# New places for the routing matmuls among the expert matmuls, and one copy moved from ScalarE to VectorE

## The chip, the cores and the metric

The kernel runs on one core of one Trainium2 chip. The metric is the device time of one execution in microseconds, as a median of three runs. One core has five engines that run their own queues in order: TensorE (PE in the rows, its weight loads PEld), VectorE (DVE), ScalarE (ACT), GpSimd (POOL) and SyncE (SP, which here only issues transfers).

## The reference

Three layers follow one another on 4 x 768 = 3072 tokens of width 512. First a decaying linear attention with 8 heads of 64. Then a dense feed-forward layer, and last a layer of 8 experts:

```python
h = x @ w_in                                   # 512 -> 2048
g = h * np.tanh(softplus(h))
x = g @ w_out                                  # 2048 -> 512
logits = x @ w_gate                            # 8 experts
order = np.argsort(-logits.flatten())
for idx in order:                              # best pairs first
    tok, e = (int(idx) // E, int(idx) % E)
    if assigned[tok] >= 0 or counts[e] >= cap: # cap = 3072 / 8 = 384
        continue
    assigned[tok] = e
    counts[e] += 1
for e in range(E):
    mask = assigned == e
    out[mask] = np.maximum(x[mask] @ w1[e], 0.0) @ w2[e]
```

Every expert gets exactly 384 tokens, and which expert is filled first depends on all logits.

## The kernel before, in words

All large products are done in half precision with a high and a low part of each operand, three matmuls for each product (`mm3`, L524). The last part of the kernel, from the logits on, is what matters here. Three kinds of work run in it side by side.

The **routing** is done in eight rounds (`route_round`). Each round finds the expert that fills up next, by a search over the digits of the logits. A round r has five digit steps. In each, VectorE compares (`against`, L677, into the tile `ld`), TensorE counts with 24 small matmuls (tile `pc{r}x{0,2,4,6,8}x`, L720), VectorE thresholds (L722), TensorE spreads the result with one matmul (tile `pn{r}x{1,3,5,7,9}x`, L725), and VectorE takes the maximum (L727) and prepares the next digit (L731, L732, L734, L677). Then VectorE closes the round: it finds the number of the expert (up to L760), TensorE makes prefix sums (`pp{r}x10x`, L769 and L770), VectorE takes the chosen tokens out of the logits (up to L784), and the next round begins with L687. A side chain (`route_list`) makes the list of the 384 tokens, with 24 small matmuls (`pl{r}x11x`, L812). Rounds are strictly one after the other.

The **weights** of the expert that round r has found are fetched by two indirect transfers of 2 MB (`weights`, L855, `w1p` and `w2p`), which need the number from L760. ScalarE sums their squares (four times L861 for each), TensorE and VectorE make a scale from it (`pt{r}x2x` for w1, `pt{r}x3x` for w2, L184, L186), and ScalarE, GpSimd and VectorE split each of the eight pieces of 128x1024 into high and low parts (L213, L215, L221, L222, L227, L228).

The **experts** (`expert`) are the matmuls themselves. Expert r starts when its tokens are gathered (`prep_x`, L883) and its w1 is split. It makes eight groups of 12 matmuls of 128x384 (first half) and three groups of 24 matmuls of 128x512 (second half), into the accumulators `ph` and `px` by turns. Each group of the first half is followed by VectorE (L914), ScalarE (L915) and GpSimd (L916).

In what order TensorE and ScalarE do all this is fixed when the program is written out: `Weave` counts a planned time, adds the planned cost of each piece of main matmuls, and lets a side chain issue its next step when its planned wait has passed. For the routing, this wait is a constant of the step plus an entry of the table `KN['rs']`, one row for each round: entries 0 to 9 stand ahead of the ten matmul steps `pc`, `pn`, `pc`, ..., entry 10 ahead of `pp` and entry 11 ahead of `pl`:

```python
yield max(0.0, KN['rw'][i] + (4 if i == 0 else 1) * slack + rs[2 * i]), 0.0
pc = ps.tile([128, E], F32, name=f"pc{r}x{2 * i}x", tag="py")
```

A larger entry puts the step behind more expert matmuls in TensorE's queue. TensorE takes its queue in order: where a routing matmul stands too early, TensorE waits for VectorE with expert matmuls behind it; where it stands too late, VectorE waits. The orders of VectorE and GpSimd are made by the scheduler from the dependences.

Expert 0's tokens are special: they are transposed by TensorE (L895, three accumulators `ph`, `px`, `ph`) and copied to the tile `xt` (L897 and L899). Those of the later experts are transposed by transfers.

Of the kernel before, what the change touches and what calls it, by code (L numbers as in the profile page):

```python
# [16 lines left out]
AF = mybir.ActivationFunctionType  # L17
# [80 lines left out]
def moe_kernel(ctx, tc, qkv, w_in, w_out, w_gate, w1p, w2p,  # L98
               c_mask, c_g, c_gv, c_gs, out, dbg=None):
    nc = tc.nc  # L100
    V, A, P, T, SY = nc.vector, nc.scalar, nc.gpsimd, nc.tensor, nc.sync
# [60 lines left out]
    def first_loads():  # L162
        for x in KN['lo']:
            if x[0] == 'c':
                load_chunk(0, int(x[1]), 3 if x == 'c0' else 1)
            elif x == 'g':
                SY.dma_start(GQ, c_g)
                SY.dma_start(GV, c_gv)
            elif x == 'm':
                SY.dma_start(MASK, c_mask)  # L170
            elif x == 's':
                SY.dma_start(GS, c_gs)
            elif x == 'wg':
# [103 lines left out]
    def win_setup(q):  # L277

        zs = [RAW[:, i * 1024:i * 1024 + 1024] for i in (2 * q, 2 * q + 1)]
        for j in range(2):  # L280
            with tc.high_priority(offset=KN['cp'][q]):
              to_f32(zs[j], WIN_RAW[2 * q + j], KN['ci'][2 * q + j])
            if 2 * q + j < 3:
                win_load(2 * q + j + 5)
        yield KN['wv'][0], 0.0
        yield KN['wv'][1], 1.0
        ss = col("ssi")
        norm(zs, ss)
        yield KN['wv'][2], 0.2
        sw = pow2(total(ss, 1, "toti"), "swin", 4)  # L290
# [544 lines left out]
    def ps_any():  # L835
        return next(banks)()
# [41 lines left out]
    def prep_x(r):  # L878
        xt = wk.tile([128, 2, KD, G], F16, name="xt", tag="xt", bufs=2)
        XTE_[r] = xt  # L880
        for c in range(CPG):
            xg = XG[(r % 2) * CPG + c]
            P.indirect_dma_start(out=xg, out_offset=None, in_=xbuf,  # L883
                                 in_offset=bass.IndirectOffsetOnAxis(ap=IDX[r][:, c:c + 1], axis=0))
            if r:
                turned(xt, c, xg[:, :2 * DM])
        if r == 0:

            yield 10.0, 0.0
# [12 lines left out]

# [173 lines left out]
    wv = Weave(tc)  # L1076
# [133 lines left out]
```

## Time and profile before

| | |
|---|---|
| median of 3 runs | 1168.45 us (1164.66 to 1170.23) |
| the profiled execution's own time | 1161.92 us |
| its span, first to last instruction | 1160.1 us |
| mean granted clock of TensorE | 0.926 of full speed |
| TensorE busy | 990.7 us, 85% |
| VectorE, ScalarE, GpSimd busy | 71%, 55%, 50% |

The profile is of one execution, whose time lies 6.5 us under the median. The span is 1.8 us shorter than this execution's time. Times in the rows count from the first instruction. "Granted clock" is the share of 2.4 GHz at which TensorE was allowed to run; its two levels are 1.2 and 2.4 GHz. The brackets at the end of a row give the idle time of the engine just before and who ended it.

### The profile page before, as it was taken

What the parts mean: (1) busy time and instruction counts of PE and PEld (TensorE: products, weight loads), DVE (VectorE), ACT (ScalarE), POOL (GpSimd) and SP (SyncE); (2) the same over time, 40 slices, a digit from 0 to 9 for tenths busy, and PEclk for the clock granted to TensorE, in tenths of its full rate; (3) what the DMA queues carried; (4) which work ended last, traced back from release to release, by engine and by line L of the source; (5) the groups of instructions that cost most, each with busy time, mean ns of one, the idle gap of its engine ahead of it and who ended that gap; (6) DMA issues with size and microseconds to landing.
All of it is one profiled execution on the core that took longest, in us unless ns stands there. A gap on an engine that the chain in (4) does not pass through costs nothing. (4 is left out here: it accounts for less than half of the span.)

```text
span 1160.1 us, 19911 instructions
## 1 busy us (share of the span) xinstructions
PE 990.7 (85%) x7897; PEld 565.1 (49%) x7897; DVE 818.3 (71%) x1766; ACT 641.3 (55%) x942; POOL 585.7 (50%) x415
## 2 busy tenths in 40 slices
PE   3458768899999999999999899994888788869997
PEld 2335444445556555555565464442444444435553
DVE  6899989853777667767867465786878788695320
ACT  4336857563567575675675672153445454556741
POOL 5956463641445536335544232033476665767872
PEclk9959979889999999999999999995888889889999
DMA  9360361273130231131341100516252535527600
GB/s 302 127 185 18 137 172 29 74 138 71 47 94 17 83 74 46 37 83 47 83 79 42 37 1 20 200 28 197 91 167 82 146 119 182 154 74 182 200 28 28
DMA packets 108814, 113.67 MB, mean 98 GB/s; under 512 B 92464, under 2 KB 92592, under 8 KB 106672
## 3 DMA queue, kind: packets, MB, share of 16 engines
q1 hardware_dynamic: 102576, 66.24, 22.4%
q0 software_dynamic: 6144, 46.15, 11.6%
q8 instruction: 62, 1.02, 0.4%
q14 instruction: 32, 0.26, 0.1%
HBM read 77.50 MB, written 13.64 MB: 79 GB/s over the span
## 5 line engine op out<-in xcount | busy, mean ns | idle before, releaser
L524 PE MATMUL ph<-xt,WIN 128*128 128x384 f16 x1728 | 335.9, 336 | 7.3 <-DMA xt<-yh 3.8
L524 PE MATMUL px<-WOUT,G 128*128 128x512 f16 x1248 | 315.2, 388 | 0.2 <-DVE WOUT L228 0.2
L524 PEld LDWEIGHTS <-WIN 128*128 128x128 f16 x1920 | 188.9, 102 | 154.4 <-issue 29.7
L524 PEld LDWEIGHTS <-G 128*128 128x128 f16 x1728 | 166.5, 100 | 193.7 <-issue 20.8
L576 POOL TENSOR_TENSOR G<-RAW,G 128x1536 f16<-128x1536 f32 (+1 forms) x32 | 99.5, 3108 | 103.2 <-DVE G L573 87.2
L405 POOL TENSOR_TENSOR amt<-amt 128x512 f16<-128x512 f32 x40 | 55.7, 1393 | 121.6 <-DVE amt L402 104.9
L916 POOL TENSOR_TENSOR G<-G,G 128x384 f16<-128x384 f32 x64 | 64.7, 1017 | 70.3 <-ACT G L915 65.6
L554 DVE TENSOR_SCALAR RAW<-ph 128x384 f32<-128x384 f32 x124 | 68.1, 551 | 40.5 <-PE ph L524 39.9
L915 ACT ACTIVATE G<-G 128x384 f16<-128x384 f32 x64 | 33.0, 519 | 89.7 <-DVE G L914 89.1
L561 ACT ACTIVATE RAW<-RAW,zt,ch 128x1536 f32<-128x1536 f32 x32 | 53.3, 1665 | 48.5 <-DVE RAW L554 43.0
L324 ACT ACTIVATE junk<-ld 128x512 bf16<-128x512 f32 x63 | 39.4, 626 | 62.0 <-DMA ld<-in_qkv_dram 61.0
L570 DVE TENSOR_TENSOR RAW<-RAW 128x1536 f32<-128x1536 f32 (+1 forms) x33 | 60.6, 1837 | 15.5 <-ACT RAW L569 15.4
L222 POOL TENSOR_TENSOR RAW<-ld,RAW 128x512 f16<-128x512 f32 x34 | 45.6, 1357 | 50.9 <-ACT RAW L221 45.9
L861 ACT ACTIVATE junk<-RAW 128x1024 bf16<-128x1024 f32 x64 | 67.1, 1048 | 6.7 <-DMA RAW<-in_w1p_dram,MASK 6.0
L677 DVE TENSOR_TENSOR ld<-MASK,ld 128x1536 bf16<-128x1536 bf16 (+1 forms) x35 | 56.5, 1614 | 0.7
L222 POOL TENSOR_TENSOR STH<-SC,STH 64x256 f16<-64x256 f32 x34 | 32.0, 942 | 42.2 <-ACT STH L221 39.1
L524 PEld LDWEIGHTS <-WOUT 128*128 128x128 f16 x384 | 38.7, 104 | 27.5 <-issue 6.1
L399 DVE TENSOR_TENSOR amt<-pa,MASK 128x512 f32<-128x512 f32 x38 | 26.1, 688 | 35.1 <-PE pa L398 30.6
L524 PE MATMUL px<-WIN,G 128*128 128x512 f16 x192 | 44.3, 380 | 5.8 <-POOL G L916 3.1
L720 PEld LDWEIGHTS <-ld 128*128 128x128 bf16 x840 | 24.8, 97 | 49.7 <-DVE ld L677 46.8
L222 POOL TENSOR_TENSOR WIN<-RAW,WIN 128x1024 f16<-128x1024 f32 x19 | 45.3, 2389 | 5.5 <-ACT WIN L221 5.3
L569 ACT ACTIVATE RAW<-RAW 128x1536 f32<-128x1536 f32 (+1 forms) x33 | 47.7, 1445 | 0.4
(585 smaller groups left out, 2145.5 us busy)
## 6 DMA issues: line engine op xcount, KB each, us to landing
ld<-in_qkv_dram SPq DMA_DIRECT2D x20, 768.0 KB, 4.9
G<-in_w_in_dram SPq DMA_DIRECT2D x8, 1024.0 KB, 8.5
G<-in_w_out_dram SPq DMA_DIRECT2D x8, 1024.0 KB, 5.3
x_rows<-xr SPq DMA_DIRECT2D x24, 256.5 KB, 2.8
G<-in_qkv_dram SPq DMA_DIRECT2D x2, 768.0 KB
g_columns<-G SPq DMA_DIRECT2D x1, 1024.0 KB
G<-g_columns SPq DMA_DIRECT2D x1, 1024.0 KB
ld<-in_qkv_dram SPq DMA_DIRECT2D x3, 256.0 KB, 2.8
```

Of the source, the lines that this page charges most:

```text
L222: (V if pool in ("V", "E") else P).tensor_tensor(lo, src, hi, op=OP.subtract)
L324: A.activation(junk(), x.rearrange("p a d -> p (a d)"), AF.Square, accum_out=ss[:, i:i + 1])
L405: (P if mode[1] == "P" else V).tensor_tensor(amh[:, j, 1], am, amh[:, j, 0], op=OP.subtract)
L524: T.matmul(p, a, b, start=i == 0, stop=i == n - 1)
L554: V.tensor_scalar(hs[:, f], p[:, :G], 1.0 / 65536.0, None, op0=OP.mult)
L561: A.activation(th, hs, AF.Tanh, scale=ch[:, q:q + 1], bias=z)
L569: A.activation(th[:, w], th[:, w], AF.Sin, scale=-2.0, bias=math.pi / 2)
L570: (V if hm[1] == 'V' else P).tensor_tensor(th[:, w], th[:, w], hs[:, w], op=OP.mult)
L576: (P if lo == 'P' else V).tensor_tensor(gb[:, 1, o], th[:, w], gb[:, 0, o], op=OP.subtract)
L677: V.tensor_tensor(out.rearrange("p t (j v) -> p t j v", v=VR), cv[:, ts, None, :].to_broadcast([128, n, J // VR, VR]), RT["jr128"][:, :J]. ...
L861: A.activation(junk(1024), RAW[:, o:o + 1024], AF.Square, accum_out=ss[:, j:j + 1])
L916: P.tensor_tensor(hid[:, 1, f], hs, hid[:, 0, f], op=OP.subtract)
```

## The change

Two things are changed. The rows 0 to 7 of the table `rs` get new entries, 67 of 96; and all three copies of expert 0's transposed tokens are done by VectorE, where ScalarE did the second one. The row of round 3 shows the size of the first:

```diff
-rs=[...
-[0.56, 0.0, 0.38, 0.0, 0.15, 0.0, 0.12, -0.11, -0.04, -0.27, 0.03, -3.34],
+rs=[...
+[1.97, 0.0, -0.9, -0.59, 4.52, 0.43, 0.84, -0.56, 3.53, 0.17, -0.61, -4.08],
...
-                if c == 1:
-                    A.activation(xt[:, :, :, c * C:(c + 1) * C], p, AF.Copy)
-                else:
-                    V.tensor_copy(xt[:, :, :, c * C:(c + 1) * C], p)
+                V.tensor_copy(xt[:, :, :, c * C:(c + 1) * C], p)
```

The number of instructions and their operands stay the same on TensorE; only places differ. In the changed kernel the lines behind L896 have numbers that are 3 lower.

**First place: TensorE, round 3, from the spreading matmul of the second digit to the counting matmuls of the third.** The first column of names is the accumulator, with its running number. Before:

```order
L725 MATMUL pn3x3x_9375<-MASK_83,onesb_77 128x8
L524 LDWEIGHTS G1_68
L524 MATMUL px_9320<-WIN_64,G1_68 128x512
...
L524 MATMUL ph_9394<-xt_9022,WOUT_65 128x384
L720 LDWEIGHTS ld_7847
L720 MATMUL pc3x4x_9410<-MASK_83,ld_7847 128x8
```

After the change:

```order
L725 MATMUL pn3x3x_9390<-MASK_83,onesb_77 128x8
L524 LDWEIGHTS WOUT_65
L524 MATMUL ph_9385<-xt_8994,WOUT_65 128x384
...
L524 MATMUL px_9456<-xt_8994,WOUT_65 128x384
L720 LDWEIGHTS ld_7847
L720 MATMUL pc3x4x_9472<-MASK_83,ld_7847 128x8
```

Before, 4 matmuls of 128x512 and 12 of 128x384 stood between the two; now 44 of 128x384 do, the last of them for the fourth group of expert 1.

**Second place: the weights of expert 6.** GpSimd issues the transfers, and TensorE's matmuls `pt6x2x` and `pt6x3x` sum the squares of w1 and w2. GpSimd before, from the issue for w1 to the issue for w2:

```order
L855 DMA RAW_66<-in_w1p_dram,MASK_83 128x4096
L916 TENSOR_TENSOR G1_68<-G0_67,G1_68 128x384 x3
L215 TENSOR_SCALAR RAW_66<-RAW_66,se1_11271 128x1024 x2
L222 TENSOR_TENSOR WOUT_65<-RAW_66,WOUT_65 128x1024
L916 TENSOR_TENSOR G1_68<-G0_67,G1_68 128x384
L222 TENSOR_TENSOR WOUT_65<-RAW_66,WOUT_65 128x1024 x2
L883 DMA G0_67<-x2_rows,GQ_81 128x1026 x3
L933 DMA out_0_dram<-G0_67,GQ_81 3072x512
L855 DMA RAW_66<-in_w2p_dram,MASK_83 128x4096
```

GpSimd after (L913 is the line that was L916):

```order
L855 DMA RAW_66<-in_w1p_dram,MASK_83 128x4096
L913 TENSOR_TENSOR G1_68<-G0_67,G1_68 128x384 x2
L855 DMA RAW_66<-in_w2p_dram,MASK_83 128x4096
L913 TENSOR_TENSOR G1_68<-G0_67,G1_68 128x384
```

TensorE after, where expert 6 begins:

```order
L812 LDWEIGHTS amt_7848
L812 MATMUL pl7x11x_11665<-GQ_81,amt_7848 128x6
L184 MATMUL pt6x2x_11692<-sse0_11412,onesf_79 128x4
L184 MATMUL pt6x3x_11706<-sse1_11414,onesf_79 128x4
L524 LDWEIGHTS WIN_64
L524 MATMUL px_11730<-xt_11628,WIN_64 128x384
```

The two issues now stand next to each other, and both sums stand directly ahead of expert 6's first matmul. Before, `pt6x2x` stood among the first groups of expert 5 and `pt6x3x` in its second half.

**Third place: VectorE, the copies of expert 0's tokens.** Before, with ScalarE's copy of `px` (L897) in another queue:

```order
L899 COPY xt_8735<-ph_8851 128x8x128
L734 TENSOR_TENSOR MASK_83<-MASK_83 128x192
L191 TENSOR_SCALAR se0a_8844<-tote_8842 128x1
L923 TENSOR_SCALAR GQ_81<-G0_67,ie_8696 128x1
L677 TENSOR_TENSOR ld_7847<-MASK_83,ld_7847 128x24x64
L899 COPY xt_8735<-ph_8871 128x8x128
```

After:

```order
L896 COPY xt_8735<-ph_8840 128x8x128
L734 TENSOR_TENSOR MASK_83<-MASK_83 128x192
L896 COPY xt_8735<-px_8850 128x8x128
L677 TENSOR_TENSOR ld_7847<-MASK_83,ld_7847 128x24x64
L896 COPY xt_8735<-ph_8860 128x8x128
```

The scale of expert 1's weights (L191), which stood between the copies, now comes behind them.

## Rows read from the trace of the kernel before

**Rows 1.** The page, busy time of the engines over the span.
```profile
PE 990.7 (85%) x7897; PEld 565.1 (49%) x7897; DVE 818.3 (71%) x1766; ACT 641.3 (55%) x942; POOL 585.7 (50%) x415
```

**Rows 2.** Windows: length; busy PE, PEld, DVE, ACT, POOL; granted clock, DMA share, GB/s.
```profile
797.00:1060.00 263.00, 214.47 (x1640) 113.73 (x1640) 203.43 (x541) 126.26 (x188) 165.20 (x121) 0.86 0.45 134
1060.00:1147.00 87.00, 86.02 (x468) 45.41 (x466) 27.93 (x49) 51.32 (x77) 61.75 (x50) 1.00 0.37 113
```

**Rows 3.** Waits of TensorE, 797 to 1060 us: total, times, longest.
```profile
PE px L524 <- ACT xt L897: 4.0, 1, 4.0
PE pc3x4x L720 <- DVE ld L677: 4.0, 1, 4.0
...
PE pc6x4x L720 <- DVE ld L677: 2.2, 1, 2.2
```

**Rows 4.** Timeline of TensorE, around the third digit of round 3.
```profile
858.24 0.80 PE L720 MATMUL pc3x4x<-MASK,ld 128*128 128x8 bf16 x24 [4.00 <-DVE ld L677]
...
859.32 2.72 PE L524 MATMUL px<-xt,WOUT 128*128 128x384 f16 x8
861.98 0.18 PE L725 MATMUL pn3x5x<-MASK,onesb 64*128 64x8 bf16 x1
```

**Rows 5.** Timeline of TensorE, the last groups of expert 7.
```profile
1134.38 2.11 PE L524 MATMUL px<-xt,WOUT 128*128 128x384 f16 x12
1136.33 5.34 PE L524 MATMUL ph<-WOUT,G 128*128 128x512 f16 x24
1141.51 5.34 PE L524 MATMUL px<-WOUT,G 128*128 128x512 f16 x24
1146.68 5.34 PE L524 MATMUL ph<-WOUT,G 128*128 128x512 f16 x24
```

**Rows 6.** Timeline of all engines where expert 0 begins.
```profile
803.60 0.69 DVE L899 COPY xt<-ph 128x1024 f16<-128x1024 f16 x1 [1.13 <-PE ph L895]
...
805.44 1.00 ACT L897 ACTIVATE xt<-px 128x1024 f16<-128x1024 f16 x1
...
806.50 4.00 PE L524 MATMUL px<-xt,WIN 128*128 128x384 f16 x12 [4.01 <-ACT xt L897]
...
811.57 0.81 PE L720 MATMUL pc2x4x<-MASK,ld 128*128 128x8 bf16 x24
```

**Rows 7.** Timeline of TensorE, the last digit step of rounds 2, 5 and 6.
```profile
829.21 0.18 PE L725 MATMUL pn2x9x<-MASK,onesb 64*128 64x8 bf16 x1
...
969.09 0.18 PE L725 MATMUL pn5x9x<-MASK,onesb 64*128 64x8 bf16 x1
...
1020.88 0.19 PE L725 MATMUL pn6x9x<-MASK,onesb 64*128 64x8 bf16 x1
```

**Rows 8.** Timeline of GpSimd, the issue of w1 for expert 6.
```profile
1026.68 0.97 POOL L855 DMA_INDIRECT RAW<-in_w1p_dram,MASK  x1 [2.75 <-DVE MASK L760]
```

**Rows 9.** The transfers of L855: from issue to landing.
```profile
DMA to landing us min/median/max: 8.6/8.8/13.0
```

**Rows 10.** Groups by line and form, 797 to 1147 us: count, busy us, mean ns.
```profile
L861 ACT ACTIVATE junk<-RAW 128x1024 bf16<-128x1024 f32 x52 | 54.4, 1047 | 1.2 <-DMA RAW<-in_w1p_dram,MASK 0.7
...
L222 POOL TENSOR_TENSOR WOUT<-RAW,WOUT 128x1024 f16<-128x1024 f32 x18 | 39.8, 2219 | 4.0 <-ACT WOUT L221 3.8
...
L228 DVE SCALAR_TENSOR_TENSOR WOUT<-RAW,se,WOUT 128x1024 f16<-128x1024 f32 x14 | 22.5, 1606 | 5.8 <-ACT WOUT L227 5.7
...
L914 DVE TENSOR_SCALAR G<-ph 128x384 f32<-128x384 f32 x32 | 17.7, 554 | 23.5 <-issue 8.6 <-PE ph L524 8.5 <-POOL G L916 3.2
...
L227 ACT ACTIVATE WOUT<-RAW,se 128x1024 f16<-128x1024 f32 x14 | 15.9, 1138 | 25.2 <-DVE se L194 25.2
```

**Rows 11.** Timeline of all engines, a routing step on VectorE beside GpSimd.
```profile
813.92 2.13 POOL L222 TENSOR_TENSOR WOUT<-RAW,WOUT 128x1024 f16<-128x1024 f32 x1 [1.25 <-ACT WOUT L221]
...
814.39 1.70 DVE L731 SCALAR_TENSOR_TENSOR MASK<-MASK 128x24 bf16<-128x24 bf16 x1
...
824.37 0.26 DVE L731 SCALAR_TENSOR_TENSOR MASK<-MASK 128x24 bf16<-128x24 bf16 x1
```

More of the change, by code (lines that the diff above doesn't have):

```diff
@@ L36 @@
 DIGITS = ((25, 7), (18, 7), (12, 6), (6, 6), (0, 6))
-KN = dict(ea=1, sc=1, pw=4, le=0.0, hl=['P', 'P'], cs=['V', 'V', 'V', 'V', 'V', 'V', 'V'], cc=['V', 'V', 'V', 'V', 'V', 'V', 'V', 'V', 'V'], lo=['c0', 'g', 'c1', 'm', 'c2', 's', 'wg', 'w0', 'w1', 'w2'], ga=['', 'V'], rs=[[-0.63, 0.3, -1.2, 0.0, 0.24, 0.0, 0.09, 0.0, 0.21, 0.0, 0.0, -4.24], [2.1, 0.09, 2.19, 0.0, 0.58, 0.15, 0.18, 0.15, 0.26, 0.26, 1.46, -0.41], [3.26, 0.0, -0.68, 0.2, 0.33, 0.0, -0.3, 0.0, 0.09, -0.12, 0.3, -3.18], [0.56, 0.0, 0.38, 0.0, 0.15, 0.0, 0.12, -0.11, -0.04, -0.27, 0.03, -3.34], [0.67, 0.0, 0.31, -0.76, 0.89, 0.0, 0.15, -0.22, 0.0, 0.0, -0.16, -4.15], [1.46, -2.35, 0.04, -0.29, 0.13, -2.18, 0.42, -0.4, 0.45, 0.03, 1.16, -4.07], [0.45, 0.54, 0.45, 0.0, 1.18, 0.0, -0.39, -0.55, -0.61, -0.05, 0.45, -3.57], [-0.15, 0.0, -0.75, 0.0, 0.0, 0.0, 0.0, -0.3, 0.0, 0.0, 3.28, -3.01]], fs=[[0.0, 0.0, -3.96, -1.22], [-0.75, 0.0, 1.32, 0.16], [0.0, 0.0, -2.08, 0.13], [0.0, -1.13, 0.71, 0.36], [0.0, 0.0, 0.0, -0.56], [0.38, 0.75, 0.13, 0.04], [0.0, 0.38, 0.2, 0.69], [0.0, -1.5, -0.61, 0.29]], av=[5.75, 5.75, 2.0, 4.0], a2=[1.3, 2.2, 4.3], a1=[0.1, 1.0, 0.85], ao=[3.5, 3.5, 3.35], wv=[8.5, 0.5, 1.0, 4.5], ov=5.0, an=[3.0, 3.15, 3.6], qm=['P0', 'VP', 'VP', 'PH', 'P1', 'VV', 'VP'], vm=['P0', 'VP', 'VP', 'VP', 'VP', 'P0', 'VP'], km=['A', 'H', 0, 0, 0, 0, 0], am=['VP', 'VP', 'VP', 'AV', 'VP', 'AV', 'VP'], ss=['V', 'P', 'P', 'P', 'P', 'P', 'P'], sm=['P', 'V', 'V', 'P', 'E', 'D', 'P'], ym=[0, 0, 0], hm=['VVVP', 'VVAV', 'VVVP', 'VVVP', 'AVVP', 'VVVP', 'VVVP', 'VVVP', 'VVVP'], ci=['PP', 'PP', 'AP', 'PP', 'PP', 'PP', 'VP', 'PP'], co=['AP', 'PP', 'PP', 'PP', 'AP', 'PP', 'PP', 'PP'], wa=[15, 12, 8, -1, 7, 16], cp=[0, 100, 0, 100], np=0, yp=[0, 2000], op=[0, 0, 200, 0, 50, 1000], xp=[0, 0, 0, 0, 0, 0], ld=[0, 1, 2, 3, 4], wj=[4, 4, 4], fw=[13.5, 18.5, 14, 16, 14, 16], qs=1.0, tw=3.0, sw=1.5, po=[[0, 1, 0, 1, 0, 0, 0, 1], [0, 'A', 0, 1, 0, 1, 0, 0], [0, 1, 0, 1, 0, 1, 0, 1], [0, 'A', 0, 'A', 'A', 1, 0, 1]], sl=[0, 0, 0.7], rw=[4.9, 2.5, 1.55, 1.7, 1.7], pn=0.5, lw=14.0, gx=9.0, tk=2.75, st=[16.0, 21.0, 20.0, 23.5], wi=['H', 'A', 0, 0, 2, 0, 0, 0], wo=['H', 'H', 0, 0, 0, 0, 'H', 0], tp=[], gw=5.15, nw=1.0, cw=0, sp=50, ap=1000, wp=None, ip=None)
@@ new lines @@
+KN = dict(ea=1, sc=1, pw=4, le=0.0, hl=['P', 'P'], cs=['V', 'V', 'V', 'V', 'V', 'V', 'V'], cc=['V', 'V', 'V', 'V', 'V', 'V', 'V', 'V', 'V'], lo=['c0', 'g', 'c1', 'm', 'c2', 's', 'wg', 'w0', 'w1', 'w2'], ga=['', 'V'], rs=[[-0.17, 0.3, 0.32, 0.0, 0.24, -0.1, 0.09, -0.1, 0.51, -0.1, -0.52, -4.58], [2.1, 1.0, 0.74, 0.0, 0.99, -0.62, 1.08, 2.0, -0.2, 0.16, -0.44, -0.41], [3.26, 0.0, -0.99, 0.2, 0.69, -0.45, 3.77, 0.43, 0.09, -0.57, 0.3, -4.61], [1.97, 0.0, -0.9, -0.59, 4.52, 0.43, 0.84, -0.56, 3.53, 0.17, -0.61, -4.08], [2.13, -0.19, 1.72, -0.76, 4.94, 0.44, -0.63, -0.67, 2.68, 0.44, 0.84, -3.66], [3.09, -0.58, 0.04, -0.99, 0.13, -1.79, 1.61, 0.18, 2.13, -0.42, 3.65, -3.58], [0.95, 0.94, -0.23, -0.7, 3.7, 0.43, -0.39, -0.55, 2.89, 0.38, 0.45, -3.11], [-0.15, 0.0, -0.75, 0.0, 0.0, 0.0, 0.0, -0.3, 0.0, 0.0, 3.91, -6.01]], fs=[[0.0, 0.0, -3.96, -1.22], [-0.75, 0.0, 1.32, 0.16], [0.0, 0.0, -2.08, 0.13], [0.0, -1.13, 0.71, 0.36], [0.0, 0.0, 0.0, -0.56], [0.38, 0.75, 0.13, 0.04], [0.0, 0.38, 0.2, 0.69], [0.0, -1.5, -0.61, 0.29]], av=[5.75, 5.75, 2.0, 4.0], a2=[1.3, 2.2, 4.3], a1=[0.1, 1.0, 0.85], ao=[3.5, 3.5, 3.35], wv=[8.5, 0.5, 1.0, 4.5], ov=5.0, an=[3.0, 3.15, 3.6], qm=['P0', 'VP', 'VP', 'PH', 'P1', 'VV', 'VP'], vm=['P0', 'VP', 'VP', 'VP', 'VP', 'P0', 'VP'], km=['A', 'H', 0, 0, 0, 0, 0], am=['VP', 'VP', 'VP', 'AV', 'VP', 'AV', 'VP'], ss=['V', 'P', 'P', 'P', 'P', 'P', 'P'], sm=['P', 'V', 'V', 'P', 'E', 'D', 'P'], ym=[0, 0, 0], hm=['VVVP', 'VVAV', 'VVVP', 'VVVP', 'AVVP', 'VVVP', 'VVVP', 'VVVP', 'VVVP'], ci=['PP', 'PP', 'AP', 'PP', 'PP', 'PP', 'VP', 'PP'], co=['AP', 'PP', 'PP', 'PP', 'AP', 'PP', 'PP', 'PP'], wa=[15, 12, 8, -1, 7, 16], cp=[0, 100, 0, 100], np=0, yp=[0, 2000], op=[0, 0, 200, 0, 50, 1000], xp=[0, 0, 0, 0, 0, 0], ld=[0, 1, 2, 3, 4], wj=[4, 4, 4], fw=[13.5, 18.5, 14, 16, 14, 16], qs=1.0, tw=3.0, sw=1.5, po=[[0, 1, 0, 1, 0, 0, 0, 1], [0, 'A', 0, 1, 0, 1, 0, 0], [0, 1, 0, 1, 0, 1, 0, 1], [0, 'A', 0, 'A', 'A', 1, 0, 1]], sl=[0, 0, 0.7], rw=[4.9, 2.5, 1.55, 1.7, 1.7], pn=0.5, lw=14.0, gx=9.0, tk=2.75, st=[16.0, 21.0, 20.0, 23.5], wi=['H', 'A', 0, 0, 2, 0, 0, 0], wo=['H', 'H', 0, 0, 0, 0, 'H', 0], tp=[], gw=5.15, nw=1.0, cw=0, sp=50, ap=1000, wp=None, ip=None)
```

## The prediction, made before the changed kernel ran

> **What bounds the kernel now.** I read the page first, then windows, then TensorE's waits, then the timelines at the places where the order changes. TensorE is busy for 85% of the span, more than any other engine [rows 1], but not evenly. From 1060 us on it is busy for 86.02 of 87 us at a granted clock of 1.00: experts 5, 6 and 7 run there as fast as they can. From 797 to 1060 us, where experts 0 to 4 share the queue with rounds 2 to 7 of the routing, it is busy for 214.47 of 263 us at 0.86 [rows 2]. The reader should see that this second stretch is the only one with something to gain, and that there the routing sets the pace: in the list of waits nearly all the long ones are a counting matmul that waits for VectorE's comparison (L677), 4.0 us at the worst. Six of them in rounds 3 to 6 are over 2 us, from 4.0 down to 2.2 [rows 3].
>
> A wait costs twice. Behind the 4.00 us ahead of `pc3x4x`, the 8 expert matmuls up to `pn3x5x` took 2.66 us, from 859.32 to 861.98 [rows 4]; 12 of the same size take 1.95 us at the full clock, from 1134.38 to 1136.33 [rows 5], so 8 take 1.30. The routing itself, which stands behind them, came 1.36 us late.
>
> At the full clock a whole expert is 8 x 1.95 + 3 x 5.18 = 31.1 us [rows 5]. That is my unit for counting places in the order.
>
> **What the new table does.** The step `pc3x4x` now has 44 matmuls ahead of it where 16 stood. The 44 are 7.2 us of work at the rates above; the 16 were 2.8, and with the wait of 4.00 [rows 4] VectorE was ready after 6.8. So it goes in all rounds: counted in the two orders, TensorE does 38.1 us of expert work between the first steps of rounds 3 and 4 (31.2 before), 41.0 in the next round (30.3), 35.3 in the one after (28.6). By the last digit of round 6 (`pn6x9x`) the experts are at 165.1 us of their work instead of 132.6. If the routing kept its times, the whole 32 us would be gained. It will not, for three reasons that I cost in turn.
>
> **Round 2, and the copy.** TensorE waits 4.01 us for ScalarE's copy of `px`, which ran from 805.44; the third copy, on VectorE, was done at 803.60 + 0.69 = 804.3. With all three on VectorE, expert 0 begins at about 804.4 instead of 806.50: -2.1 [rows 6]. Its price is one copy of 0.69 us on VectorE, in a stretch where VectorE waited 1.13 us for the third transpose. Then `pc2x4x` has 8 matmuls ahead where it had 16; at the pace of those rows (4.00 for 12, against 2.11 in [rows 5]) that is another -2.5. Together -4.6 for the routing.
>
> **The clock.** The six long waits in rounds 3 to 6 go, if the places fit. Each gives the routing back about 1.36 us of slow matmuls: -8. The lower bound is 0, if other waits of this length take their place.
>
> **VectorE's work.** The 32.5 us of expert work moved ahead are 1.04 experts. One expert is 8 instructions L914 of 0.55 us and some 4 of L228 of 1.6 us [rows 10], 10.8 us of VectorE, or 11 for the share that is moved. None of it matters if it falls into idle time, all of it if it stands ahead of the routing's next step. VectorE is busy for 203.43 of 263 us [rows 2], so I take +8 of 0 to 11.
>
> **The weights of experts 4 to 7.** Here lies the new cost. Before, the two transfers of an expert were issued far apart and long ahead. Now the experts have caught up with the routing, and both are issued as soon as the round has named its expert, next to each other. From `pn6x9x` the chain is: 5.8 us to the issue of w1, 1020.88 to 1026.68 [rows 7, 8]; 2.5 for the two GpSimd instructions up to the issue of w2; 13.0 to its landing, the longest of the measured ones, as two transfers share the engines (8.8 is the median, and the lower bound) [rows 9]; 7 for the six sums of squares that stand in ScalarE's order behind the first one of w2, 1.05 each and a short read; 1 for the scale; 9.9 for the nine pieces of ScalarE's split up to the last of w1, 1.05 to 1.14 each; 2.2 for the last low part on GpSimd [rows 10]. That is 41 to 42 us. Expert 4 stands 32.9 us of expert work behind `pn4x9x`, and the routing steps in between, the slowest of a round, bring that to some 41, so there is hardly a wait (+1). Expert 5 stands 29.9 behind `pn5x9x`, with some 5 of routing matmuls, and waits 7, and the second half of round 6 stands behind expert 5's first matmuls, so that the routing pays these 7 too. Expert 6 stands 22.1 and 3 behind `pn6x9x` and waits 17.
>
> **The sum.** For the routing up to `pn6x9x`: -4.6 - 8 + 8 + 1 + 7 = +3.4, so about 1024.3 instead of 1020.88. From there to the end of the last matmul it was 1146.68 + 5.18 - 1020.88 = 131.0 us [rows 5, 7]. Now it is 42 to the first matmul of expert 6, 62.2 for two experts, 7 for expert 7 (its w1 is issued only behind four of the five low parts of expert 6 on GpSimd, its w2 5 us later, and the same 13 + 6 + 1 + 10 + 2 follow: 39 us after the start of expert 6, where TensorE is ready at 32), and 2 x 1.8 for the slow clock after these two waits (12 matmuls in 4.00 instead of 2.11 [rows 6]). That is 115: -16. In all 3.4 - 16 = **-12.6 us**. The profiled execution took 1161.92 us and lies 6.5 under the median; I put the same gain on both, so 1149 for its like and 1156 for the median of the runs.
>
> Rounds 0 and 1, where steps move by about 1 us, I cost at nothing: round 2's first step waits for VectorE, and expert 0 for its gather, in either order. If that cover were gone, it would be 1 or 2 us either way.
>
> **Rival 1, slower: VectorE is blocked by GpSimd more often.** A short step of the routing, L731, takes 0.26 us alone but took 1.70 while GpSimd worked on a low part of 2.13 us, from 813.92; it ended at 816.09, with GpSimd at 816.05 [rows 11]. More expert work in the routing's rounds means more such low parts in them. If each of the 20 short digit steps of rounds 2 to 6 meets one more, for half of its 2.2 us on average, the routing loses 22 us and the result is -12.6 + 22 = +9, about 1178. It decides the sign from 12.6 us on, that is from a little over half of the steps. Against it speaks that much of this blocking is already in the steps measured before. The Trainium skill, on the page "SBUF — State Buffer", section "SBUF: two separate sides", says that GpSimd and a two-input VectorE instruction share one pair of ports as an exclusive lock for a whole instruction. By that rule every meeting costs, never a part; the 0.04 us between the two ends agrees.
>
> **Rival 2, no change: the weights set the pace from round 5 on.** If the chain of 42 us is 50, because ScalarE has evictions and L915 ahead of the squares, expert 4 waits 7, expert 5 another 8, and experts 6 and 7 together some 8 to 10 more, partly overlapping: about +13 and so 0, near 1168. For it speaks that in the new order the squares of expert 5 stand behind all eight L915 of expert 4. Against it, that these are done before w2 lands.
>
> **Rival 3, a larger gain.** VectorE's added work falls into idle time (-8) and w2 lands 8.8 us after its issue (-4 at expert 6): -24, about 1144.
>
> That the change does not do what it says, so that waits of the old size come back at other steps, is part of rival 2: the gain of the clock (-8) is lost and the tail pays the rest.
>
> **Chances.** The forecast 0.45, between -20 and -4; rival 1 0.25; rival 2 0.17; rival 3 0.13. Half a per cent, about 5.8 us, is what a measurement of this kernel can tell. Faster by more: 0.40 of the forecast's 0.45, all of rival 3 and nothing else, 0.53. Slower by more: nearly all of rival 1 and a little of rival 2, 0.27. Within: 0.20. The range 1142 to 1180 reaches from beyond rival 3 to rival 1 and leaves out the tails of both; the forecast's own range is 1148 to 1165.
>
> **What would show it.** In the new trace the waits of TensorE for L677 should nearly all be under 1.5 us, and the granted clock between 841 and 985 us should be near 0.95. Expert 0's first matmul should start near 804.4. `pn6x9x` should come within 1015 to 1035. TensorE should wait more than 10 us in front of expert 6 and some 7 in front of experts 5 and 7, with ScalarE's squares and splits (L861, L221) or GpSimd's low parts named as the releasers, and the window behind `pn6x9x` should be about 16 us shorter. The prediction is wrong if the routing stretches: should `pn6x9x` come later than 1036, nothing is gained whatever the tail does. It is also wrong, to the other side, if there is no wait ahead of expert 6, since then the pair of transfers is cheaper than I think.

## The result, and the profile after

The changed kernel is slower: 1186.94 us median of 4 runs (1180.68 to 1188.02) against 1169.34 us for the kernel before; the ratio is 1.014, with a 95% interval of 1.0106 to 1.0175. The forecast was 1156 us. The profiled execution took 1186.84 us with a span of 1185.1; the one of before (1161.92 us) lay 7.4 us under this median, so the two spans differ by 25.0 us where the medians differ by 18.

The page of the changed kernel, busy time of the engines (the row that answers to [rows 1]): TensorE has 5 us more, VectorE and GpSimd have 4 and 10 less, ScalarE is the same.

```profile
PE 996.0 (84%) x7897; PEld 566.4 (48%) x7897; DVE 814.1 (69%) x1767; ACT 641.6 (54%) x941; POOL 575.8 (49%) x415
```

Timeline of TensorE in the changed kernel, the steps of [rows 4 to 7]. Expert 0's first matmul and `pc2x4x`; `pc3x4x`; the last digit step of rounds 2, 5 and 6; the last group of expert 7.

```profile
804.95 2.72 PE L524 MATMUL px<-xt,WIN 128*128 128x384 f16 x8 [0.95 <-DVE xt L896]
807.47 0.80 PE L720 MATMUL pc2x4x<-MASK,ld 128*128 128x8 bf16 x24
...
827.22 0.18 PE L725 MATMUL pn2x9x<-MASK,onesb 64*128 64x8 bf16 x1
...
860.49 0.75 PE L720 MATMUL pc3x4x<-MASK,ld 128*128 128x8 bf16 x24
...
992.87 0.16 PE L725 MATMUL pn5x9x<-MASK,onesb 64*128 64x8 bf16 x1 [5.36 <-DVE MASK L722]
...
1059.07 0.18 PE L725 MATMUL pn6x9x<-MASK,onesb 64*128 64x8 bf16 x1
...
1171.66 5.34 PE L524 MATMUL ph<-WOUT,G 128*128 128x512 f16 x24
```

Against [rows 7] `pn2x9x` is 2.0 us earlier, `pn5x9x` 23.8 later and `pn6x9x` 38.2 later. From there to the end of the last matmul it is 1171.66 + 5.34 - 1059.07 = 117.9 us, where it was 131.0: 13.1 less. So 38.2 were lost in the routing and 13.1 won back in the tail, which makes the 25.

**What the routing's stretch holds.** I take the stretch from behind the start of `pc2x0x` to `pp7x10x`, rounds 2 to 6. First the windows of the kernel before: all engines, then the matmuls L524 (experts) alone.

```profile
789.91:1030.75 240.84, 193.41 (x1562) 104.75 (x1560) 190.15 (x505) 117.06 (x176) 149.19 (x107) 0.85 0.44 132
...
789.91:1030.75 240.84, 169.66 (x768) 77.58 (x768) 0.85 0.44 132
```

The same windows of the changed kernel; the last row is the window 841 to 985 us.

```profile
791.16:1068.68 277.52, 227.59 (x1743) 122.93 (x1740) 197.40 (x525) 126.81 (x190) 161.63 (x125) 0.87 0.45 119
...
791.16:1068.68 277.52, 206.69 (x948) 95.36 (x948) 0.87 0.45 119
...
841.00:985.00 144.00, 124.55 (x969) 66.67 (x966) 103.68 (x267) 77.44 (x115) 88.05 (x69) 0.92 0.42 124
```

The reader should see that the stretch grew by 36.7 us, and that the expert matmuls in it took 37.0 us more (206.69 - 169.66). Every microsecond of work put into it was paid in full. The waits of TensorE say why. Its longest waits in the stretch, in the changed kernel:

```profile
PE pc6x6x L720 <- DVE ld L677: 6.4, 1, 6.4
PE pn5x9x L725 <- DVE MASK L722: 5.4, 1, 5.4
PE px L524 <- POOL G L913: 5.2, 2, 3.2
PE pl1x11x L812 <- DVE amt L677: 3.9, 3, 1.9
PE pc2x8x L720 <- DVE ld L677: 3.3, 1, 3.3
PE pc3x6x L720 <- DVE ld L677: 3.2, 1, 3.2
```

The waits of [rows 3] are gone from their places: `pc3x4x`, `pc3x8x`, `pc4x4x`, `pc4x8x`, `pc6x4x` and `pc6x8x` wait for nothing. Others have come. All rows for matmuls of the routing together were 41.1 us before and are 37.2 now; those for expert matmuls rose from 5.8 to 12.4. Of the list of before, three more of the waits that are gone:

```profile
PE pc4x4x L720 <- DVE ld L677: 3.7, 1, 3.7
PE pc3x8x L720 <- DVE ld L677: 3.2, 1, 3.2
PE pc6x8x L720 <- DVE ld L677: 3.2, 1, 3.2
```

So 37.0 - 3.9 + 6.6 = 39.7 us, which is the added length but for 3.0 us of overlap.

**Where VectorE stands.** For each of the 54 steps in the stretch I took from the timelines when VectorE was done for it and when TensorE reached it. VectorE's own time, from the end of the step before, fell from 164.7 to 151.3 us in all. The time by which TensorE came after VectorE rose from 46.2 to 95.2. The plainest case is the step that the prediction started from. VectorE's comparison for `pc3x4x` and GpSimd beside it, before:

```profile
854.82 3.36 DVE L677 TENSOR_TENSOR ld<-MASK,ld 128x1536 bf16<-128x1536 bf16 x1
855.22 2.13 POOL L222 TENSOR_TENSOR WOUT<-RAW,WOUT 128x1024 f16<-128x1024 f32 x1
```

And in the changed kernel:

```profile
853.87 0.97 POOL L855 DMA_INDIRECT RAW<-in_w2p_dram,MASK  x1 [0.30 <-issue]
...
854.66 0.96 DVE L677 TENSOR_TENSOR ld<-MASK,ld 128x1536 bf16<-128x1536 bf16 x1
```

The same comparison takes 3.36 us beside a low part on GpSimd and 0.96 beside none. The new entry for `pc3x4x` had been made for the first; with the new order the low part lies elsewhere, VectorE is ready at 855.62, and TensorE reaches the step at 860.49, 4.9 us late. It is the other way round where the waits are now. At `pn5x9x`, VectorE and GpSimd in the changed kernel:

```profile
985.30 7.45 DVE L228 SCALAR_TENSOR_TENSOR WIN<-RAW,se,WIN 128x1024 f16<-128x1024 f32 x1
985.38 6.27 POOL L222 TENSOR_TENSOR WIN<-RAW,WIN 128x1024 f16<-128x1024 f32 x3
...
992.67 0.15 DVE L722 TENSOR_SCALAR MASK<-pc5x8x 64x8 bf16<-64x8 f32 x1
```

A low part on VectorE (L228), 1.28 us where nothing disturbs it, takes 7.45 beside three on GpSimd in a row; the routing's L722 stands behind it in VectorE's queue, and TensorE waits 5.36 us.

How much of the longer stretch hangs on this can be estimated from the two traces: take each of the 54 steps as the larger of VectorE's own time and TensorE's work up to it, and leave out the waits of expert matmuls. That gives 204 us for the kernel before and 232 for the changed one. With VectorE's times of before and the new work of TensorE it gives 214. So some 10 us of the 28 come from entries that were too large already for the old times, and some 18 from VectorE's times that moved to other steps, although their sum fell.

**The tail.** TensorE's waits of the changed kernel behind 1068.68 us:

```profile
PE ph L524 <- POOL WOUT L222: 7.1, 2, 5.4
PE px L524 <- DVE WIN L228: 6.8, 2, 6.2
PE px L524 <- POOL WIN L222: 3.7, 1, 3.7
PE ph L524 <- ACT G L912: 2.5, 1, 2.5
```

Expert 7 waits 7.1 us for low parts on GpSimd, expert 6 for both kinds: at its longest wait VectorE's two L228 and GpSimd's four L222 lie beside each other, and TensorE stands behind them:

```profile
1091.29 0.82 PE L524 MATMUL px<-xt,WIN 128*128 128x384 f16 x2 [1.23 <-ACT WIN L227]
...
1095.74 8.35 POOL L222 TENSOR_TENSOR WIN<-RAW,WIN 128x1024 f16<-128x1024 f32 x4
...
1096.56 9.81 DVE L228 SCALAR_TENSOR_TENSOR WIN<-RAW,se,WIN 128x1024 f16<-128x1024 f32 x2 [3.93 <-ACT WIN L227]
...
1097.91 1.14 PE L524 MATMUL px<-xt,WIN 128*128 128x384 f16 x3 [3.66 <-POOL WIN L222]
...
1105.23 1.14 PE L524 MATMUL px<-xt,WIN 128*128 128x384 f16 x3 [6.19 <-DVE WIN L228]
```

### The profile page after: what moved, and what is told of

Same layout as the page of the kernel before. It is cut to its first block, busy times and chain, and to the rows that moved or that the text cites. A ratio compares the mean times of both kernels' runs of the same rounds, so it can differ in the third digit from the quotient of the medians.

```text
span 1185.1 us, 19914 instructions
## 1 busy us (share of the span) xinstructions
PE 996.0 (84%) x7897; PEld 566.4 (48%) x7897; DVE 814.1 (69%) x1767; ACT 641.6 (54%) x941; POOL 575.8 (49%) x415
## 4 chain that ended last, share of the span: by engine, by line
PE 50%; DVE 24%; issue 9%; POOL 8%; ACT 4%; DMA 4%; POOLq 0%; SPq 0%; ACTq 0%; DVEq 0%
PE px L524 21%; PE ph L524 20%; DVE WIN L228 2%; DVE WOUT L228 1%; PE py L433 1%; POOL G L913 1%; POOL WOUT L222 1%; DVE ld L677 1%; POOL amt L405 1%; DVE RAW L570 1%; DMA xt<-yh 1%; DVE ld L372 1%; DVE RAW L554 1%; DVE MASK L731 1%; PE pa L396 1%
## 5 line engine op out<-in xcount | busy, mean ns | idle before, releaser
L524 PE MATMUL ph<-xt,WIN 128*128 128x384 f16 x1728 | 336.3, 337 | 7.3 <-DMA xt<-yh 3.8
L524 PE MATMUL px<-WOUT,G 128*128 128x512 f16 x1248 | 317.3, 390 | 0.6 <-DVE WOUT L228 0.6
L524 PEld LDWEIGHTS <-WIN 128*128 128x128 f16 x1920 | 189.0, 102 | 175.9 <-issue 38.6
L524 PEld LDWEIGHTS <-G 128*128 128x128 f16 x1728 | 167.3, 101 | 193.5 <-issue 24.6
L913 POOL TENSOR_TENSOR G<-G,G 128x384 f16<-128x384 f32 x64 | 61.8, 971 | 64.9 <-ACT G L912 64.6
L222 POOL TENSOR_TENSOR RAW<-ld,RAW 128x512 f16<-128x512 f32 x34 | 45.7, 1358 | 49.7 <-ACT RAW L221 48.0
L524 PEld LDWEIGHTS <-WOUT 128*128 128x128 f16 x384 | 39.6, 107 | 40.3 <-issue 10.4
L222 POOL TENSOR_TENSOR STH<-SC,STH 64x256 f16<-64x256 f32 x34 | 32.0, 942 | 42.2 <-ACT STH L221 39.1
L524 PE MATMUL px<-WIN,G 128*128 128x512 f16 x192 | 46.0, 386 | 6.6 <-POOL G L913 5.2
L524 PE MATMUL px<-xt,WIN 128*128 128x384 f16 x192 | 40.5, 359 | 12.8 <-DVE WIN L228 6.8
L524 PE MATMUL ph<-WOUT,G 128*128 128x512 f16 x192 | 45.8, 391 | 4.5 <-ACT G L912 2.5
L677 DVE TENSOR_TENSOR ld<-MASK,ld 128x1536 bf16<-128x1536 bf16 (+1 forms) x35 | 49.0, 1399 | 0.8
```

The costliest lines, as they stand in the source:

```text
L222: (V if pool in ("V", "E") else P).tensor_tensor(lo, src, hi, op=OP.subtract)
L524: T.matmul(p, a, b, start=i == 0, stop=i == n - 1)
L677: V.tensor_tensor(out.rearrange("p t (j v) -> p t j v", v=VR), cv[:, ts, None, :].to_broadcast([128, n, J // VR, VR]), RT["jr128"][:, :J]. ...
L913: P.tensor_tensor(hid[:, 1, f], hs, hid[:, 0, f], op=OP.subtract)
```

## The experiments

My first theory, **late places**: the entries of rounds 3 to 6 hold the routing's steps behind more expert work than VectorE needs time. Rivals: the loss comes from the early rounds or the copy; or VectorE and GpSimd block each other more, because more expert work stands in the rounds. After the first four kernels I sharpened the theory to **moving waits**: how long VectorE needs for a digit step hangs on which GpSimd work lies beside it, the order of the experts decides that, and so a table made from the waits of one order does not fit the order that it makes. Its rival is GpSimd's load as such. In the diffs B stands for the table of before and A for the new one (in the kernels the numbers are written out). Unless said otherwise all three copies are on VectorE.

**Which rows of the table.**

```diff
# copy_only
-rs=A
+rs=B
# rows_0_2
-rs=A
+rs=A[:3] + B[3:]
# rows_3_7
-rs=A
+rs=B[:3] + A[3:]
```

Expected of the first: 

> Before's table, with the three copies of expert 0's tokens on VectorE. Late places (theory: the loss comes from the entries of rounds 3 to 6, which hold the routing's steps behind more expert work than VectorE needs time): expert 0 begins about 2 us earlier and nothing else changes, so 1167, between -3 and 0 us against before. Early rounds (rival: the copies and rows 0 to 2 of the table cost the time): VectorE's copy delays round 2, +3 us or more. Blocking (rival: VectorE and GpSimd get in each other's way because more expert work stands in the rounds): as late places, since no expert work moves.

Expected of the second: 

> The changed kernel with before's rows 3 to 7 of the table. Late places: round 2 is as in the changed kernel, pn2x9x some 2 us earlier than before, and rounds 3 to 6 as before, so 1163 to 1170. Early rounds: most of the 18 us are lost here too, 1180 or more. Blocking: little expert work is moved, 1165 to 1172.

Expected of the third: 

> The changed kernel with before's rows 0 to 2. Late places: rounds 3 to 6 take 226 us instead of 189 as in the changed kernel, 1183 to 1190. Early rounds: near before, 1167 to 1172. Blocking: as late places, 1183 to 1190, but then with VectorE's own time between two steps of the routing longer than before, not TensorE's.

Measured: the copies alone 1166.98 us (0.9983, 0.9944 to 1.0023), no difference that can be told. Rows 0 to 2 new: 1152.69 us (0.989, 0.9838 to 0.9943), faster than I expected. Rows 3 to 7 new: 1178.68 us (1.0116, 1.0051 to 1.0181), some 5 us under the range of late places. Taken alone, the early rounds and the copies are no loss; most of it lies in the later rows. The parts do not add up, though: -1.1 and +1.2 per cent together are not +1.4. With rows 3 to 7 new, the routing's stretch was 269.3 us and TensorE's waits for it 43.4, again not less than the 41.1 of before.

**How far, and which of the later rows.**

```diff
# half_way
-rs=A
+rs=(A + B) / 2, entry by entry
# rows_0_4
-rs=A
+rs=A[:5] + B[5:]
```

Expected of the first: 

> Each entry of the table halfway between before and after. Late places: the waits that were filled are half filled, and steps that stand late do so by half as much; VectorE's own need per round (183 us in all in the changed kernel, 195 before) stays, so the routing comes out between, 1165 to 1178. Early rounds: halfway, 1178. Blocking: half of the added expert work, 1178.

Expected of the second: 

> The changed kernel with before's rows 5 to 7. Moving waits: the routing is some 15 us late at the end of round 4 as in the changed kernel, and rounds 5 and 6 add nothing; experts 0 to 3 are then ahead by what rounds 3 and 4 hold more (some 20 us), which the tail gives back if the weights allow: 1160 to 1172. If the loss sits in rounds 3 and 4: 1180.

Measured: 1159.92 us for half way (0.9943, 0.9907 to 0.9978), a little under the range that I gave, and 1171.8 us with rows 0 to 4 (1.0025, 0.999 to 1.0061), at its upper end. The first lies under both kernels, the second between them; the rows 5 to 7 make up most of the loss, and a smaller step in the same direction is no loss at all.

**The same rule once more.** Each entry of rounds 2 to 6 was corrected by what the changed kernel's trace shows: plus the wait of a step that waits, minus the lateness of one that TensorE reaches late. Round 3 as an example, whose entry for `pc3x4x` goes back to where it was:

```diff
-[1.97, 0.0, -0.9, -0.59, 4.52, 0.43, 0.84, -0.56, 3.53, 0.17, -0.61, -4.08]
+[1.67, -0.22, 1.27, -0.59, 0.09, -0.61, 3.78, -0.83, -1.18, -1.14, -0.72, -4.08]
```

Expected: 

> The entries of rounds 2 to 6 derived once more by the same rule, now from the changed kernel's own trace: a step that waited is moved back by its wait, a step that TensorE reached late is moved forward. Moving waits (theory: how long VectorE needs for a digit step hangs on which GpSimd work lies beside it, and that moves with the order, so the places never fit): TensorE's waits for the routing stay at 30 us or more in all, at other steps than before, and the time is anywhere near before's, 1160 to 1185. Once too far (rival: the first derivation was too coarse, and the next one comes closer): the waits fall under 20 us and the time under 1150.

Measured: 1189.41 us (1.0177, 1.0113 to 1.024). TensorE's waits for the routing in the stretch were 53.9 us in all, its longest:

```profile
PE pc4x4x L720 <- DVE ld L677: 6.5, 1, 6.5
PE pc4x0x L720 <- DVE ld L677: 5.5, 1, 5.5
PE pc6x8x L720 <- DVE ld L677: 5.3, 1, 5.3
```

The step `pc4x4x` waited 3.7 us before, none in the changed kernel, and 6.5 now. Neither mark of the rival was met, and the rule does not come closer to anything. It was not followed exactly: the entries of `pc3x0x` and `pc5x0x` were lowered by 0.30 and 0.79 where the trace shows TensorE 2.2 and 3.7 us late. `pc5x0x` now waits 4.1 us all the same, so a full correction would hardly have helped there. The time is 4 us over my range: the stretch shortened to 247.6 us, but only because it held less expert work (159.69 us of L524), which the tail then had to do.

**Without GpSimd's share of the splits.** In `weights`:

```diff
-                split(W[:, 0, ...], W[:, 1, ...], RAW[...], SW[i, r][0], pool=KN['po'][min(r, 3)][4 * i + j])
+                m = KN['po'][min(r, 3)][4 * i + j]
+                if m:
+                    A.activation(W[:, 0, ...], RAW[...], AF.Copy, scale=SW[i, r][0])
+                else:
+                    split(W[:, 0, ...], W[:, 1, ...], RAW[...], SW[i, r][0], pool=0)
```

Expected with the new table: 

> The changed kernel without GpSimd's share of the splits of expert weights: its scalings (L215) and its low parts (L222) are left out, the low halves of those pieces are not computed. Moving waits: with nothing of 2.2 us on GpSimd beside it, VectorE needs some 2 us for each digit step, TensorE waits for the routing 20 us or less in all, and the raised entries are plain lateness; the routing still stands behind the same expert work, so its stretch from round 2 to round 7 shortens only by the waits, some 20 to 25 us, to about 255 us, and the whole to 1160. GpSimd's load as such (rival: the added blocking is the loss): the loss of 18 us goes, and this kernel and the one with before's table come out alike.

Expected with before's: 

> Before's table with the three copies on VectorE and GpSimd's share of the splits of expert weights left out, as in the kernel ahead. Moving waits: TensorE's waits for the routing fall from 41 to 15 or less, the stretch from round 2 to round 7 shortens by some 25 us, to about 212 us, and the whole to 1145 or less, still some 15 us under the kernel ahead. GpSimd's load as such: equal to the kernel ahead.

Measured: 1122.56 us (0.9599, 0.9528 to 0.9671) and 1118.32 us (0.9577, 0.9498 to 0.9657). For the pieces marked 'A' the edit also leaves out ScalarE's scaling (L213). The windows of the stretch (all engines, then L524), with the new table:

```profile
780.87:1021.39 240.52, 214.37 (x1742) 118.33 (x1740) 161.37 (x526) 119.08 (x182) 95.95 (x91) 0.92 0.55 138
...
780.87:1021.39 240.52, 193.02 (x948) 91.30 (x948) 0.92 0.55 138
```

and with before's:

```profile
785.73:991.69 205.96, 177.67 (x1562) 99.80 (x1559) 156.71 (x506) 108.07 (x166) 88.74 (x78) 0.93 0.73 156
...
785.73:991.69 205.96, 155.10 (x768) 73.44 (x768) 0.93 0.73 156
```

The waits for the routing fell to 13.9 us, within the 20 that I gave, and to 20.6, not to the 15 that I gave. Both kernels are faster than I gave (1160, and 1145 or less). The stretch is still 34.6 us longer with the new table, for 37.9 us more work. But the whole time is the same within 0.4 per cent, against my 15 us: here the tail gives the work back. The rival is right about the totals, and half of my theory was too narrow. What the table costs is decided in the tail as well, and that too hangs on GpSimd's low parts.

**All low parts on VectorE.** Nothing is left out here but the scaling ahead of a low part on GpSimd (L215 on GpSimd, L213 on ScalarE), which VectorE's form of it does not need, so what is said of GpSimd's low parts from here on holds for both together:

```diff
-po=[[0, 1, 0, 1, 0, 0, 0, 1], [0, 'A', 0, 1, 0, 1, 0, 0], [0, 1, 0, 1, 0, 1, 0, 1], [0, 'A', 0, 'A', 'A', 1, 0, 1]]
+po=[[0]*8, [0]*8, [0]*8, [0]*8]
```

With rows 0 to 2 new: 

> The version with the new rows 0 to 2 and before's rows 3 to 7 (1152.7 us), and all low parts of expert weights on VectorE, none on GpSimd. Moving waits: no step of VectorE is stretched by a low part on GpSimd, waits fall by 10 to 20 us, but VectorE has some 23 us more of its own low parts (18 of 1.28 us) in the stretch, so 1145 to 1156. GpSimd's load as such: 1130 to 1140.

With before's table: 

> Before's table and the copies on VectorE, all low parts of expert weights on VectorE. Moving waits: GpSimd's part in the waits is gone whatever the table, so about 18 us under the same table with GpSimd (1167), 1145 to 1152. If the gain of the version with rows 0 to 2 hung on its table, it would stay at 1160 or more.

With the new table: 

> The changed kernel with all low parts of expert weights on VectorE. Moving waits, refined by the two kernels without low parts: the routing stays some 35 us later than with before's table, but without GpSimd in the chain of the weights the tail gives most of it back, so 1135 to 1155, within 10 us of the kernel ahead. If the late places cost by themselves: 1160 or more.

Half way: 

> The table halfway between both, all low parts on VectorE. The halfway table with GpSimd's low parts was at 1160 against 1153 with new rows 0 to 2; without them 18 us less, 1135 to 1145; as a candidate for the best version it should come within 1 per cent of 1134.

| table | low parts as before | all on VectorE |
|---|---|---|
| before's, copies on VectorE | 1166.98 | 1137.36 (0.9758, 0.9684 to 0.9832) |
| new rows 0 to 2 | 1152.69 | 1134.23 (0.9706, 0.9647 to 0.9765) |
| half way | 1159.92 | 1114.93 (0.9551, 0.9489 to 0.9612) |
| new | 1186.94 | 1137.99 (0.9757, 0.9685 to 0.9828) |

Only the expectation for the new table was met; in the others the gain was larger than I gave. The time with new rows 0 to 2 lies in the range that I gave to the rival, GpSimd's load as such, so the times alone do not rule this rival out. Between before's table and the new one there is now no difference: the 18 us of the change hang on the low parts on GpSimd. The estimate from step times, made in the same way for these two, gives 187 and 206 us for the two kernels, and 202 for before's times with the new work: where no low part is on GpSimd, VectorE's times that move cost some 3 us instead of 18. The routing is still 26.7 us later with the new table at `pn6x9x`, and the tail gives 25.6 back. VectorE does more than twice as many low parts and each is shorter, as are the routing's own instructions. Groups by line and form in the stretch of the changed kernel:

```profile
L677 DVE TENSOR_TENSOR ld<-MASK,ld 128x1536 bf16<-128x1536 bf16 x15 | 18.7, 1244 | 0.4
...
L228 DVE SCALAR_TENSOR_TENSOR WIN<-RAW,se,WIN 128x1024 f16<-128x1024 f32 x7 | 17.9, 2558 | 1.2 <-ACT WIN L227 1.2
...
L732 DVE TENSOR_SCALAR MASK<-MASK 128x24 bf16<-128x24 bf16 x20 | 9.8, 490 | 0.0
```

and of the fastest one (half way, low parts on VectorE), whose window of the stretch stands below them:

```profile
L228 DVE SCALAR_TENSOR_TENSOR WIN<-RAW,se,WIN 128x1024 f16<-128x1024 f32 x16 | 20.9, 1314 | 2.5 <-ACT WIN L227 2.4
...
L677 DVE TENSOR_TENSOR ld<-MASK,ld 128x1536 bf16<-128x1536 bf16 x15 | 15.4, 1028 | 0.3
...
L732 DVE TENSOR_SCALAR MASK<-MASK 128x24 bf16<-128x24 bf16 x20 | 6.5, 323 | 0.0
```

```profile
786.54:1007.87 221.33, 194.30 (x1671) 109.33 (x1669) 183.28 (x539) 114.58 (x176) 89.50 (x84) 0.96 0.49 147
```

This version beats both kernels by 4.5 per cent and more. Its waits for the routing are 23.0 us in all, its granted clock in the stretch 0.96, where the kernels before and after had 0.85 and 0.87.

**In which place the low parts cost.** The new table, with the low parts of experts 0 to 4 alone on VectorE, and with those of experts 5 to 7 alone:

```diff
-... pool=KN['po'][min(r, 3)][4 * i + j])
+... pool=KN['po'][min(r, 3)][4 * i + j] if r > 4 else 0)   # after_v_early
+... pool=KN['po'][min(r, 3)][4 * i + j] if r < 5 else 0)   # after_v_late
```

Expected of the first: 

> The changed kernel with the low parts of experts 0 to 4 on VectorE, those of experts 5 to 7 still on GpSimd. If the loss is in the digit steps (moving waits): most of the 49 us between the changed kernel (1187) and the one with all low parts on VectorE (1138) is won, 1140 to 1152. If it is in the chain of the last weights: little is won, 1165 to 1180.

Expected of the second: 

> The changed kernel with the low parts of experts 5 to 7 on VectorE, those of experts 0 to 4 still on GpSimd. Digit steps: the routing still comes to its last digit step some 30 us later than before, but the waits of TensorE for the low parts (17 us ahead of experts 5 to 7) shrink to under 8, 1165 to 1178. Chain of the last weights: 1150 or less.

Measured: 1165.04 us (0.999, 0.9947 to 1.0033) and 1167.65 us (0.9981, 0.994 to 1.0022). The first is what the chain of the last weights would give, the second what the digit steps would, so neither is the cause alone: of the 49 us between 1187 and 1138 the one wins 22 and the other 19. Before's table gains 30 of its own without the low parts on GpSimd, and was not run with one half of them moved, so how the 18 us of the change divide between the two places is not shown. With the first, `pn6x9x` comes 27.6 us sooner than in the changed kernel, and the waits for the last weights stay (7.1 us for L222 at expert 7, 6.2 and 3.7 at expert 6). With the second the routing stays where it was, `pn6x9x` 35.1 us later than before, and TensorE's waits for low parts shrink. Of its list from 1041 us on, where the only one for the routing, `pc6x6x` with 5.3 us, is left out:

```profile
PE ph L524 <- ACT G L912: 2.3, 1, 2.3
PE px L524 <- DVE WIN L228: 2.3, 2, 1.2
...
PE ph L524 <- DVE WOUT L228: 1.0, 1, 1.0
```

## Why the prediction was wrong

**The step that failed is the sum for the routing, +3.4 us up to `pn6x9x`.** It measured +38.2. Behind it stands the sentence that the six long waits go "if the places fit". I took the 32 us of expert work as filling waits and priced a misfit only by the lost clock, at most 8 us. In fact the work cost its full 37.0 us, because TensorE's waits for the routing fell by 3.9 us only. Many of them had been VectorE's stretched instructions, and these moved with the order: by the estimate above this is some 18 of the 28 us by which the steps grew, and entries too large from the start some 10. The prediction's own mark, nothing gained if `pn6x9x` comes later than 1036, was met with 1059.07.

**The copy, and round 2** (-4.6): expert 0 began at 804.95 (forecast 804.4) and `pc2x4x` came 4.1 us earlier, near the forecast (8 matmuls at 4.00 us for 12 are 2.7 us, so the term should have read -4.8). At the end of the round 2.0 were left, since `pc2x8x` now waited 3.3 us. Alone, the copy gave no gain that can be told.

**The clock** (-8): in the window 841 to 985 us it rose from 0.88 to 0.92, forecast near 0.95. The routing did not come earlier for it.

**VectorE's work** (+8): VectorE was busy 7.2 us longer in the stretch, the size that was forecast. But its time for the routing's steps fell, from 164.7 to 151.3 us, so this term did not delay the routing.

**Rival 1** named the right pair of engines and the sign, but not what happened. It wanted more meetings of VectorE with GpSimd on the digit steps. The time of these steps did not grow: in the stretch the 15 L677 took 24.4 us before and 18.7 after, the 20 L731 14.7 and 13.4, the 20 L732 7.2 and 9.8, the 20 L734 11.7 and 12.3, together 58.0 and 54.2. What grew were the low parts on VectorE, from 25.9 us for 17 to 36.1 for 18. And the stretched instructions lay at other steps, which the places did not know. That the time came out slower, as rival 1 has it, is luck as far as its sum goes.

**The tail** (-16) measured -13.1. Expert 7 waited 7.1 us (forecast 7), expert 6 some 13.5 in seven pieces (forecast 17), expert 5 3.1 (forecast 7). The two issues for expert 6 did come next to each other. Expert 6's first matmul came 1091.29 - 1059.07 = 32.2 us behind `pn6x9x`, not 42, but its longest waits, 3.66 and 6.19 us, came after it, for low parts of GpSimd and VectorE in each other's way, and the last of them ended 1105.23 - 1059.07 = 46.2 us behind. So the sum of the chain was near, but its terms were not: w2 landed 9.9 us after its issue instead of 13.0, while ScalarE's squares stood behind an eviction (L929, at 1082.00) and the low parts took what was saved. With all low parts on VectorE, the tail gives back 25.6 of 26.7.

**What stays open.** Why new rows 0 to 2 gain 14 us over before's under the old rows 3 to 7 and lose 8 under the new ones: the sums do not explain it. The traces show one reason why rows do not add up: VectorE's times for the 44 steps of rounds 3 to 6 hang on the rows ahead of them. Between the copies alone and the version with new rows 0 to 2, which share the rows 3 to 7, they differ by 47 us, summed over the steps without sign; between the kernel before and the copies alone by 8. Which of these differences make the 14 and the 8 is not shown. Also why the halfway table is the best one without low parts on GpSimd; that it is so is one measurement of one table between two, not an optimum.

## What to carry to other kernels

A wait is not a constant of the step at which it stands. Before filling it with work, look at which instruction of the waited-for engine is longer than its undisturbed twin, and what lies beside it; if that neighbour will move with the change, the wait can come back elsewhere, and the work then costs its full time, as it did here. Take the disturbing work away first (here: low parts to the engine that it disturbed, -2.5 per cent with the same table) and place the steps afterwards. And work that is moved ahead of a bottleneck is a gain only if the tail can run without it: ask what the tail waits for once it has less to do.

## What the runs showed of the hardware

VectorE's short instructions were stretched by elementwise work on GpSimd, also those with one input: L732 takes 0.23 us alone and 2.15 beside L222, L677 0.96 and up to 3.53. Beside GpSimd's issues of indirect transfers alone (L855, L883, L930) they kept their 0.23 to 0.96 us. The Trainium skill, on the page "SBUF — State Buffer", section "SBUF: two separate sides", tells of a lock for the whole of one instruction. The rows agree that it is whole, and show more: VectorE can stay blocked through several GpSimd instructions in a row. One L228 took 7.45 us beside three L222 of 6.27 in all; of the two in the row of 9.81 us, the first took 8.61 beside four L222 of 8.35 and the second 1.27. It is not always so. Five microseconds before the first of these, VectorE came in between two L222 in a row, and each of its instructions was stretched by one of them only:

```profile
979.94 2.19 DVE L732 TENSOR_SCALAR MASK<-MASK 128x24 bf16<-128x24 bf16 x1
979.96 4.21 POOL L222 TENSOR_TENSOR WIN<-RAW,WIN 128x1024 f16<-128x1024 f32 x2
...
982.17 2.21 DVE L734 TENSOR_TENSOR MASK<-MASK 128x192 bf16<-128x192 bf16 x1
```

What decides between the two is not shown. L911, which reads an accumulator of TensorE, kept 0.54 to 0.56 us whatever lay beside it.

I had not expected that VectorE, given all of GpSimd's low parts as well, would be less busy: with the new table 189.3 us in the stretch, with 40 low parts of some 1.3 us, against 197.4 with 18 of 2.0 us. The expert matmuls in it are 948 in both.
